# The last product of a three-layer kernel, computed by Strassen's algorithm in pairs of token tiles

## The chip, the cores and the metric

The kernel runs on one core of a Trainium2 chip. The metric is device time in microseconds, the median of 3 runs. One execution was profiled; times inside it are counted from its first instruction. PE is the matmul engine, PEld its weight loads, DVE, ACT and POOL the three engines for elementwise work, SP the engine that issues nearly all DMAs.

## The reference

Three layers follow each other. Here is what they compute, with shapes:

```python
# q, k, v: (4, 8, 576, 64)
kv  = einsum('bhsd,bhse->bhde', k, v)
o   = einsum('bhsd,bhde->bhse', q, kv)
x   = o / sqrt(mean(o*o) + 1e-6) * g_norm            # -> (2304, 512) tokens
h   = x @ w_in                                       # (512, 1024)
s   = h * softmax(h)
x   = layernorm(s) * g_ln @ w_out                    # (1024, 512)
out = ((x @ w_a) * (x @ w_b)) @ w_out2               # (512,1536) twice, (1536,512)
```

The last line is the part that concerns us: a = x @ w_a, b = x @ w_b, and the output product (a*b) @ w_out2 with 2304 tokens, 1536 inner columns and 512 output columns.

## The kernel before

All arithmetic is in float32. A matmul operand is split into a high part (rounded to the type fp32r by an ACT cast) and a low part (the rest, by a subtraction on DVE or POOL), and a product is three matmuls: high by high, high by low, low by high.

The products a and b run in units called quads (`quad`, L726). The 2304 tokens are three blocks s of 768 (SB = 6 tiles of 128), the 1536 inner columns are 6 groups j of 256, and m says whether a or b is made. A quad already uses Strassen's algorithm: a 2 by 2 arrangement of half blocks is multiplied by 7 products (`product`, L706, 6 matmuls of 384 columns each) and 15 sums and differences instead of 8 products. The sums of x and of the weights are made beforehand; the sums of results are the `add` calls on DVE. The seventh product of a quad is issued within the next quad (`close_quad`), after that quad's third. In m = 1 the results are multiplied with those of m = 0 (`times`, mostly on POOL) and stored to DRAM in `gd[s]`.

The output product (`mm_out`, L824) is plain. For each of 18 token tiles it accumulates 12 chunks of 128 inner columns, three matmuls each, into one PSUM bank of 512 columns: 36 matmuls, 648 in all. The token tile is the stationary operand, the weight w_out2 (512 columns) the moving one. Its operands come back from `gd` two tiles at a time (`g_fetch`), and are split by one ACT cast and one DVE subtraction of 1536 columns for each tile (`g_steps`). The weight is loaded and split during the last four quads (`wo_steps`, as side steps).

Nothing reorders the program: each engine executes its instructions in the order in which the Python code issues them. A quad calls `tick` after six of its products. At each tick it issues a share of a list of side steps (`side`) and whatever `delayed` holds for that tick, so that work which is not the quad's own is placed between its own instructions. An instruction that waits holds up everything behind it on its engine; a DMA that waits holds up SP's later DMAs. `first_place`, `second_place` and `last_place` take over memory of tiles that are no longer needed.

PSUM has six banks for these stages; a quad uses three (b1, b2, b3) and hands them to the next but one.

Of the kernel before, what the change touches and what calls it, by code (L numbers as in the profile page):

```python
# [19 lines left out]
P = 128  # L20
# [79 lines left out]
def tile_attention_moe(ctx, tc, q, k, v, g_norm, w_in, w_out, g_ln, w_a, w_b, w_out2, out):  # L100
# [58 lines left out]
    pool("lp", 1).tile([P, 168], F32, name="lp")  # L159
# [8 lines left out]
    ring = xl0.tile([P, 7 * TB // 2], I64, tag="x", name="ring")  # L168
# [72 lines left out]
    def put_w2(f, eng, c):  # L241
        nc.sync.dma_start(out=w2d[c], in_=f)
# [331 lines left out]
    def x_begin(s):  # L574

        t = xl0.tile([P, 7, 2, TH], F32, tag="x", name="xf")
        x_load(s, [t[:, n] for n in (XB11, XT3, XB21, XB22)])

        def minus(out, a, b):
            return lambda: subtract(nc.vector, t[:, out], t[:, a], t[:, b])  # L580
# [32 lines left out]
    def stage():  # L613

        t = xl0.tile([P, 7 * TB // 2], I64, tag="x", name="st")
        st.update(wr=t[:, :2 * DM], wu=t[:, 2 * DM:3 * DM], ws=t[:, 3 * DM:3 * DM + 3 * P], e=t[:, 3 * DM + 3 * P:])
# [109 lines left out]
    def quad(j, s, m, side=()):  # L726
# [23 lines left out]
        def times(n, by, eng):  # L750

            eng.tensor_tensor(out=a[n], in0=by, in1=a[n], op=ALU.mult)  # L752
            i, h = n // 10 - 1, n % 10 - 1
            nc.sync.dma_start(out=gd[s][:, j, i, h * TH:(h + 1) * TH], in_=a[n])
# [31 lines left out]
        def close():  # L786
            product(b3, w, x, WA22, XT4, False, True)
            add(t[21], b3)
            if m:
                times(21, t[21], nc.gpsimd)  # L790
# [3 lines left out]

    wo2 = {}

    def wo_fetch(c, t):
        for k in range(2):
            wo2[c + k] = t[:, k, 0], t[:, k, 1]
            nc.sync.dma_start(out=t[:, k, 1].bitcast(F32), in_=w2d[c + k])  # L800

    def wo_steps(c, eng):
        return [
            lambda: nc.scalar.copy(wo2[c][0], wo2[c][1].bitcast(F32)),
            lambda: subtract(eng, wo2[c][1], wo2[c][1].bitcast(F32), wo2[c][0].bitcast(F32)),
        ]

    graw = {}
    gs = {}

    def g_fetch(s, n, t=None):
        if t is None:
            t = p2["gr"].tile([P, NF2, 2 * P], F32, tag="gr", name="gr")
        nc.sync.dma_start(
            out=t, in_=gd[s].rearrange("p j i t -> p (j i) t")[:, :, n * 2 * P:(n + 1) * 2 * P]
        )
        graw[s, n] = t

    def g_steps(s, n, h, where, tag="gs"):
        t = where.tile([P, 2, NF2, P], F32R, tag=tag, name="gs")  # L820
        hi, lo = gs[s, n, h] = t[:, 0], t[:, 1]
        return split_steps(hi, lo, graw[s, n][:, :, h * P:(h + 1) * P], nc.vector)

    def mm_out(s, n, h, within=None):  # L824
        hi, lo = gs.pop((s, n, h))
        po = banks["pool"].tile([P, 512], F32, tag="t", name="pq")

        order = [(k, c) for c in range(NF2) for k in range(3)]
        if within:
            order.sort(key=lambda kc: kc[0] == 2)  # L830
        for i, (k, c) in enumerate(order):
            if within and i == 12:
                within()
            wh, wl = wo2[c]
            x, w = ((hi, wh), (hi, wl), (lo, wh))[k]
            nc.tensor.matmul(po, x[:, c], w, start=(i == 0), stop=(i == len(order) - 1))  # L836
        o = p2["o"].tile([P, DM], F32, tag="o", name="o_sb")
        nc.scalar.copy(o, po)  # L838
        a = 0
# [231 lines left out]
```

## Time and profile before

| | us |
|---|---|
| median of 3 runs (lowest, highest) | 725.02 (724.25, 727.12) |
| the profiled execution | 724.55 |
| its span, first to last instruction | 722.8 |
| PE busy in the span | 693.4 (96%) |
| DVE, ACT, POOL busy | 421.4, 269.1, 298.4 |

A matmul's time in a row is its whole passage through the array; consecutive matmuls overlap, so the pace of PE is read from the distance between starts. The shares of the other engines are averages over stages that differ much.

### The profile page before, as it was taken

The page shows a single profiled execution, that of the slowest core. Times are in us where ns is not written, and L with a number is a line of the kernel's source. Part 1 is how long each engine was busy: PE and PEld are TensorE (multiplying, and loading weights), DVE is VectorE, ACT ScalarE, POOL GpSimd, SP SyncE. Part 2 cuts the span into 40 slices and gives each one's busy share as a digit, 9 for nine tenths or more (in the row PEclk, how much of TensorE's full clock was granted, in tenths as well). Part 3 has the DMA queues.
Part 4 walks back from the last instruction along what each step waited for, and adds up shares of the span by engine and source line. Part 5 has one row for each costly group of instructions (what it writes and reads, how often), then busy time and mean ns, then how long its engine had stood idle before and what let it go on. Part 6 is the DMA issues. An engine that isn't in the chain of part 4 may idle for free.

```text
span 722.8 us, 10923 instructions
## 1 busy us (share of the span) xinstructions
PE 693.4 (96%) x4064; PEld 636.1 (88%) x4064; DVE 421.4 (58%) x767; ACT 269.1 (37%) x456; POOL 298.4 (41%) x445
## 2 busy tenths in 40 slices
PE   3699999999999999999999999999999899999998
PEld 2578898998998998899999999999999788888886
DVE  3888977765688777777764565645645521221110
ACT  4558864443553346443221212223113322222230
POOL 2588776677657220124357444665444300000000
PEclk9899999999999999999999999999999999999999
DMA  9976545445532411351333331343115474433301
GB/s 295 310 229 186 186 121 181 120 131 165 164 110 67 143 41 53 116 165 56 132 112 124 114 103 55 102 135 104 44 71 196 161 250 151 147 117 116 117 34 39
DMA packets 93236, 95.08 MB, mean 132 GB/s; under 512 B 28416, under 2 KB 82688, under 8 KB 93184
## 3 DMA queue, kind: packets, MB, share of 16 engines
q1 hardware_dynamic: 88000, 89.67, 39.1%
q10 hardware_dynamic: 5184, 4.72, 1.9%
q8 instruction: 32, 0.52, 0.3%
q14 instruction: 20, 0.16, 0.1%
HBM read 65.54 MB, written 28.84 MB: 131 GB/s over the span
## 4 chain that ended last, share of the span: by engine, by line
PE 77%; DVE 7%; POOL 5%; DMA 5%; issue 4%; ACT 2%; SPq 1%; ACTq 0%; POOLq 0%; DVEq 0%
PE pw L711 27%; PE pq L836 20%; PE x2p L529 4%; PE x2p L528 4%; PE x2p L527 4%; PE ph L440 3%; PE ph L442 3%; PE ph L441 3%; PE ltp L497 2%; PE kvp L344 2%; PE po L378 1%; DMA vr<-in_v_dram 1%; DMA both<-gd 1%; POOL a L752 1%; DMA ks<-in_k_dram 1%
## 5 line engine op out<-in xcount | busy, mean ns | idle before, releaser
L711 PE MATMUL pw<-xh,wh 128*128 128x384 f32 x504 | 170.0, 337 | 1.5 <-DVE b L741 0.8
L711 PE MATMUL pw<-xh,wl 128*128 128x384 f32 x504 | 168.5, 334 | 0.0
L711 PE MATMUL pw<-xl,wh 128*128 128x384 f32 x504 | 168.5, 334 | 0.0
L836 PE MATMUL pq<-wq,gs 128*128 128x512 f32 x540 | 125.8, 389 | 2.0 <-ACT gs L558 2.0
L836 PEld LDWEIGHTS pq<-wq,gs 128*128 128x128 f32 x540 | 101.3, 188 | 23.2 <-ACT gs L558 2.3
L752 POOL TENSOR_TENSOR a<-b,a 128x384 f32<-128x384 f32 x54 | 60.9, 1140 | 120.9 <-DVE b L741 75.7
L711 PEld LDWEIGHTS pw<-xh,wh 128*128 128x128 f32 x504 | 94.6, 188 | 5.6 <-DVE b L741 2.7
L711 PEld LDWEIGHTS pw<-xl,wh 128*128 128x128 f32 x504 | 94.6, 188 | 0.0
L711 PEld LDWEIGHTS pw<-xh,wl 128*128 128x128 f32 x504 | 94.6, 188 | 0.0
L554 DVE TENSOR_TENSOR gs<-gr,gs 128x1536 fp32r<-128x1536 f32 x16 | 28.1, 1759 | 99.7 <-ACT gs L558 99.7
L527 PE MATMUL x2p<-lh,woh 128*128 128x256 f32 x288 | 82.4, 286 | 0.2 <-ACT lh L507 0.2
L528 PE MATMUL x2p<-ll,woh 128*128 128x256 f32 x288 | 80.4, 279 | 0.7 <-DVE ll L510 0.7
L529 PE MATMUL x2p<-lh,wol 128*128 128x256 f32 x288 | 80.4, 279 | 0.5 <-DVE wol L49 0.5
L442 PE MATMUL ph<-wih,xl 128*128 128x512 f32 x144 | 56.4, 392 | 1.4 <-DVE xl L425 1.4
L440 PE MATMUL ph<-wih,xh 128*128 128x512 f32 x144 | 57.0, 396 | 0.0
L441 PE MATMUL ph<-wil,xh 128*128 128x512 f32 x144 | 56.2, 391 | 0.4 <-DVE wil L49 0.4
L528 PEld LDWEIGHTS x2p<-ll,woh 128*128 128x128 f32 x288 | 54.1, 188 | 1.1 <-DVE ll L510 1.1
L527 PEld LDWEIGHTS x2p<-lh,woh 128*128 128x128 f32 x288 | 54.1, 188 | 0.8 <-ACT lh L507 0.5
L529 PEld LDWEIGHTS x2p<-lh,wol 128*128 128x128 f32 x288 | 54.0, 188 | 0.9 <-DVE wol L49 0.9
L66 POOL TENSOR_SCALAR nu<-nu 128x512 f32<-128x512 f32 x23 | 44.2, 1931 | 20.6 <-ACT nu L61 19.7
L838 ACT COPY o_sb<-pq 128x512 f32<-128x512 f32 x18 | 10.6, 588 | 107.3 <-issue 86.8
L741 DVE TENSOR_TENSOR a<-pw,a 128x384 f32<-128x384 f32 x54 | 29.7, 554 | 31.0 <-PE pw L711 30.9
(123 smaller groups left out, 1158.4 us busy)
## 6 DMA issues: line engine op xcount, KB each, us to landing
gd<-a SPq DMA_DIRECT2D x72, 192.0 KB, 1.8
gr<-gd SPq DMA_DIRECT2D x8, 1536.0 KB, 6.9
ring<-in_moe_w_out_dram SPq DMA_DIRECT2D x20, 512.0 KB, 5.4
ks<-in_k_dram SPq DMA_DIRECT2D x8, 512.0 KB, 7.0
vs<-in_v_dram SPq DMA_DIRECT2D x8, 512.0 KB, 7.6
ring<-in_moe_w_in_dram SPq DMA_DIRECT2D x8, 512.0 KB, 6.6
qs<-in_q_dram SPq DMA_DIRECT2D x16, 256.0 KB, 6.6
x2d<-x2s ACTq DMA_DIRECT2D x32, 128.0 KB, 1.8
```

Source lines behind the costliest of these rows:

```text
L66: eng.tensor_scalar(out=u, in0=u, scalar1=2.0 ** -15, scalar2=122879.9921875, op0=ALU.max, op1=ALU.min)
L440: nc.tensor.matmul(ph[:, n, :], xh[:, c, :], wh, start=(c == 0), stop=False)
L441: nc.tensor.matmul(ph[:, n, :], xh[:, c, :], wl, start=False, stop=False)
L442: nc.tensor.matmul(ph[:, n, :], xl[:, c, :], wh, start=False, stop=(c == NK - 1))
L527: nc.tensor.matmul(pa, wh[:, cs], lh[:, f, :], start=(f == 0), stop=False)
L528: nc.tensor.matmul(pa, wh[:, cs], ll[:, f, :], start=False, stop=False)
L529: nc.tensor.matmul(pa, wl[:, cs], lh[:, f, :], start=False, stop=(f == NF1 - 1))
L554: eng.tensor_tensor(out=out, in0=a, in1=b, op=ALU.subtract)
L711: nc.tensor.matmul(out, wt_[:, wn, c], xt_[xn][:, c], start=first and c == n == 0, stop=c == 1 and n == 2, skip_group_check=not first,)
L741: nc.vector.tensor_tensor(out=t, in0=ps, in1=t, op=ALU.add)
L752: eng.tensor_tensor(out=a[n], in0=by, in1=a[n], op=ALU.mult)
L836: nc.tensor.matmul(po, x[:, c], w, start=(i == 0), stop=(i == len(order) - 1))
```

## The change

The output product is now also computed by Strassen's algorithm. Two token tiles that lie 384 tokens apart in a block form a pair (9 pairs). The inner columns are halved by the two 128-column chunks of each j (6 chunks per half), the output columns into 256 and 256. A pair is 7 products of 6 chunks by 3 matmuls of 256 columns (`out_product`): 126 matmuls, 1134 in all. The results are joined by five DVE sums and two ACT copies per pair (`out_pair`).

The pair's operands are four loads, four differences and seven splits of 128x768 (`g_steps`); in pair k those of pair k + 1 are made, three or two steps at each of seven ticks. A load for pair k + 2 is issued right after the product of pair k that used the same memory. The sums of the weight's quarters (`w2_sums`, 4 per j) are made on DVE in six earlier quads and stored to DRAM. `gd` is laid out by quarter, so a store is three runs of 512 bytes per partition where it was one of 1536. The operands of the first pair are loaded and split during the last six quads in two pieces (`most`: 5 of the 6 chunks, `last`: the sixth); in the first pair its own last operands, the last weights and all of pair 1's operands are made.

```diff
+    def w2_sums(j, eng=nc.vector):
+        def step(n, a, b, op=ALU.subtract):
+            return lambda: eng.tensor_tensor(out=w2e_[j][:, n], in0=w2e_[j][:, a], in1=w2e_[j][:, b], op=op)
...
+        return [step(4, 2, 3, ALU.add), step(5, 4, 0), step(2, 0, 2), step(1, 1, 5), keep]
+    def g_load(k, n, c=slice(0, NJ), t=None):
+        s, m = pairs[k]
+        t = g2[k, n][1].bitcast(F32) if t is None else t
+        nc.sync.dma_start(out=t[:, c], in_=gd[s][:, (XB11, XT3, XB21, XB22).index(n), m, c])
+    def g_split(k, n, src, c=slice(0, NJ)):
+        return [
+            lambda: nc.scalar.copy(g2[k, n][0][:, c], src()[:, c]),
+            lambda: subtract(nc.vector, g2[k, n][1][:, c], src()[:, c], g2[k, n][0][:, c].bitcast(F32)),
+        ]
+    def g_steps(k):
...
+        return [
+            begin_, *sp(XB11), d(1, XB22, -1), *sp(XT1, 0), d(0, XB21, -2), *sp(XT2, 1), d(1, XB22, XT3),
+            *sp(XB21), *sp(XB22), *sp(XT3, 1), *sp(XT4, 0),
+        ]
+    def out_product(ps, k, wn, xn, first):
+        (wh, wl), (xh, xl) = wo2[wn], g2[k, xn]
+        for c in range(NJ):
+            for n, (xt_, wt_) in enumerate(((xh, wh), (xh, wl), (xl, wh))):
+                nc.tensor.matmul(
+                    ps, xt_[:, c], wt_[:, c], start=first and c == n == 0, stop=c == NJ - 1 and n == 2,
+                    skip_group_check=not first,
+                )
+    def out_pair(k, side, begin_=lambda: None):
...
+        b1 = bank_()
+        mm(b1, WA11, XB11, True)
+        begin_()
...
+        nc.scalar.copy(c21, b1)
+        tick()
+        b2 = bank_()
+        mm(b2, WS1, XT1, True)
+        add(c22, b2, c21)
+        tick()
+        b3 = bank_()
+        mm(b3, WS2, XT2, True)
+        add(c12, b3, c21)
+        close_quad()
+        tick()
+        mm(b1, WA12, XB21, False)
+        nc.scalar.copy(c11, b1)
+        tick()
+        mm(b2, WS4, XB22, False)
+        add(c12, b2)
+        tick()
+        mm(b3, WS3, XT3, False)
+        add(c22, b3)
+        store(1)
+        tick()
+        def close():
+            mm(b3, WA22, XT4, False)
+            add(c21, b3)
+            store(0)
...
     for j in range(1, NJ - 1):
         n = 2 * j + 2
-        quad(j, 0, 0, w_split(3, nc.vector) if j == 1 else ())
+        quad(j, 0, 0, w_split(3, nc.vector) if j == 1 else w2_sums(order.pop(0)))
...
-        quad(j, 2, 0, w_sums(n + 1))
+        quad(j, 2, 0, [*w_sums(n + 1), *(w2_sums(order.pop(0)) if j > 1 else ())])
...
+    then(
+        t1=early[10:12], t3=[first_place, wl(WA11, w1, 0)],
+        t4=[gl_(XB11, last), gl_(XT3, last), gl_(XB22, last), wl(WS1, w1, 1)], t5=[gl_(XB21, last)],
+    )
+    quad(j, 2, 0)
...
+    def last_places():
+        close_quad()
+        all_of([*half(WS4, 1), *half(WS3, 0)])
+        ab.close()
+        p2["o"] = pool_r("o", 5)
+        p2["e"] = pool_r("e", 1)
...
+        for n in (XB11, XT3, XB22, XB21):
+            g_load(1, n)
+        wo_load(WA22, None, w2[6])
...
+    first = [
+        *half(WS3, 1), *g_steps(1), *g_split(0, XT4, lambda: te[:, 0]), last_hi,
+        *half(WA22, 0, nc.gpsimd), *half(WA22, 1, nc.gpsimd),
+    ]
+    for k in range(len(pairs)):
+        out_pair(k, *((g_steps(k + 1) if k + 1 < len(pairs) else [],) if k else (first, last_places)))
```

How the instructions now stand is shown for three places. First PE in the output stage before, from the second part of the first tile on (`gs` is the split token tile, `wq` and `both` hold the weight):

```order
L836 MATMUL pq<-wq,gs 128x512 x8
L836 MATMUL pq<-both,gs 128x512 x4
L836 MATMUL pq<-wq,gs 128x512 x10
L836 MATMUL pq<-both,gs 128x512 x2
L836 MATMUL pq<-wq,gs 128x512 x30
L836 MATMUL pq<-both,gs 128x512 x6
L836 MATMUL pq<-wq,gs 128x512 x30
```

And PE in the output stage now, from the second product of the first pair on (`ga`, `gw`, `gxh` are token operands, `wo` weights; L886 is the matmul of `out_product`):

```order
L886 MATMUL pq<-wo_6122,ga 128x256 x18
L886 MATMUL pq<-wo_6122,gw 128x256 x18
L886 MATMUL pq<-wo_6269,gw 128x256 x54
L886 MATMUL pq<-wo_6122,gxh 128x256 x54
L886 MATMUL pq<-wo_6548,gw 128x256
L886 MATMUL pq<-wo_6269,gw 128x256
L886 MATMUL pq<-wo_6548,gw 128x256 x2
```

Each tile's 36 matmuls of 512 columns became, for two tiles, seven products of 18 matmuls of 256 columns; the first pair's seventh product (the row with `wo_6548` and those after it) stands after the second pair's third.

Second DVE at the turn from the last quad to the output stage, before (L741 and L752 are a quad's own sums and product, L554 the splits; in brackets the semaphores that an instruction waits for):

```order
L554 TENSOR_TENSOR gs<-both,gs 128x1536 [waits DMAHW5_49,Activation_49]
L741 TENSOR_TENSOR b_6237<-pw,b_6237 128x384 [waits DVE_49,PE_49]
L554 TENSOR_TENSOR both<-both 128x512 [waits DMAHW6_49,Activation_49]
L741 TENSOR_TENSOR b_6239<-pw,b_6239 128x384 [waits PE_49]
L741 TENSOR_TENSOR b_6238<-pw,b_6238 128x384 [waits PE_49,Pool_49]
L554 TENSOR_TENSOR gs<-both,gs 128x1536 [waits Activation_49]
L554 TENSOR_TENSOR gs<-gr,gs 128x1536 [waits DMAHW4_49,Activation_49]
L554 TENSOR_TENSOR gs<-gr,gs 128x1536 [waits Activation_49]
L554 TENSOR_TENSOR gs<-gr,gs 128x1536 [waits DMAHW5_49,PE_49,Activation_49]
```

And DVE there now (L745 and L756 are the last quad's sum and product, L557 splits and differences, L908 the pair's sums; `gxh`, `gxl` are pair 1's operands, `e` its differences, `o` the output tile):

```order
L745 TENSOR_TENSOR b_6301<-pw,b_6301 128x384 [waits PE_49,Pool_49]
L756 TENSOR_TENSOR a_6230<-b_6301,a_6230 128x384 [waits DVE_49]
L557 TENSOR_TENSOR wo_6269<-wo_6269 128x768 [waits Activation_49]
L557 TENSOR_TENSOR wo_6269<-wo_6269 128x768 [waits DMAHW0_49,Activation_49]
L557 TENSOR_TENSOR wo_6269<-wo_6269 128x768 [waits Activation_49]
L557 TENSOR_TENSOR e_6424<-gxl,gxh 128x768 [waits DMAHW4_49,DMAHW3_49,DMAHW5_49,DMAHW2_49,DMAHW6_49,DMAHW1_49,DMAHW7_49,DVE_49,Pool_49]
L908 TENSOR_TENSOR o_6420<-pq,o_6419 128x256 [waits PE_49]
L557 TENSOR_TENSOR gxh<-gxh 128x768 [waits DVE_49,Activation_49]
L557 TENSOR_TENSOR e_6425<-gxl,e_6424 128x768 [waits DMAHW0_49]
L557 TENSOR_TENSOR gxh<-e_6424,gxh 128x768 [waits Activation_49]
L908 TENSOR_TENSOR o_6420<-pq,o_6419 128x256 [waits PE_49]
```

Where DVE had one split per tile and nothing else, it now makes pair 1's operands; the difference into `e_6424`, which waits for loads, stands ahead of the first pair's own sum into `o_6420`.

Third SP's queue there, before:

```order
L754 DMA gd_78<-a_6166 128x384 [waits DMAHW0_49,DVE_49]
L754 DMA gd_78<-a_6167 128x384 [waits DMAHW1_49,Pool_49]
L754 DMA gd_78<-a_6169 128x384 [waits DMAHW2_49,Pool_49]
L754 DMA gd_78<-a_6168 128x384 [waits DMAHW3_49,Pool_49]
L814 DMA gr<-gd_79 128x12x256 [waits DMAHW4_49,PE_49]
L814 DMA gr<-gd_79 128x12x256 [waits DMAHW5_49]
```

And now (L758 is the store of `times`, L834 `g_load`, L828 `wo_load`):

```order
L758 DMA gd_67<-a_6228 128x3x128 [waits DMAHW1_49,DVE_49]
L758 DMA gd_67<-a_6229 128x3x128 [waits DMAHW2_49,Pool_49]
L758 DMA gd_67<-a_6231 128x3x128 [waits DMAHW3_49,Pool_49]
L834 DMA ga<-gd_68 128x768 [waits DMAHW4_49,PE_49]
L758 DMA gd_67<-a_6230 128x3x128 [waits DMAHW5_49,DVE_49]
L834 DMA gxh<-gd_68 128x768 [waits DMAHW6_49,PE_49]
L834 DMA gxl<-gd_68 128x768 [waits DMAHW7_49]
L834 DMA gxl<-gd_68 128x768 [waits DMAHW0_49]
L834 DMA gxl<-gd_68 128x768 [waits DMAHW1_49]
L828 DMA wo_6269<-w2d 128x1536 [waits DMAHW2_49]
```

The four loads of pair 1 (`gxh`, `gxl`) stand behind the last store of the last quad, `a_6230`, which waits for DVE; before, two loads of twice the tokens stood there.

## Rows read from the trace of the kernel before

**Rows 1.** The chain that ended last, shares of the span by engine and line, from the page.

```profile
PE pw L711 27%; PE pq L836 20%; PE x2p L529 4%; PE x2p L528 4%; PE x2p L527 4%; PE ph L440 3%; PE ph L442 3%; PE ph L441 3%; PE ltp L497 2%; PE kvp L344 2%; PE po L378 1%; DMA vr<-in_v_dram 1%; DMA both<-gd 1%; POOL a L752 1%; DMA ks<-in_k_dram 1%
```

**Rows 2.** Stretches of 29 to 144 us: busy time of each engine, granted clock.

```profile
core 0: us, PE busy (x) PEld busy (x) DVE busy (x) ACT busy (x) POOL busy (x), PEclk, DMA share, GB/s
495.00:539.00 44.00, 43.85 (x252) 43.23 (x251) 23.61 (x44) 9.03 (x15) 23.80 (x22) 1.00 0.23 80
539.00:568.30 29.30, 29.30 (x170) 29.12 (x168) 16.15 (x28) 8.50 (x16) 10.67 (x9) 1.00 0.60 204
...
574.90:719.10 144.20, 144.20 (x637) 119.22 (x636) 30.93 (x18) 33.59 (x34) 2.38 (x3) 1.00 0.36 123
```

**Rows 3.** PE in time (start us, us), start of the output stage, the wait before it.

```profile
567.93 0.33 PE L711 MATMUL pw<-xl,wh 128*128 128x384 f32 x1
568.10 0.34 PE L711 MATMUL pw<-xh,wl 128*128 128x384 f32 x1
570.42 3.02 PE L836 MATMUL pq<-wq,gs 128*128 128x512 f32 x12 [1.98 <-ACT gs L558]
573.74 0.44 PE L711 MATMUL pw<-xh,wh 128*128 128x384 f32 x1 [0.31 <-DVE b L741]
...
574.89 2.01 PE L836 MATMUL pq<-wq,gs 128*128 128x512 f32 x8
...
580.38 6.96 PE L836 MATMUL pq<-wq,gs 128*128 128x512 f32 x30
...
588.53 6.96 PE L836 MATMUL pq<-wq,gs 128*128 128x512 f32 x30
```

**Rows 4.** The last instructions of PE and ACT, in time.

```profile
717.74 1.52 PE L836 MATMUL pq<-both,gs 128*128 128x512 f32 x6
719.34 0.59 ACT L838 COPY o_sb<-pq 128x512 f32<-128x512 f32 x1 [7.57 <-PE pq L836]
```

**Rows 5.** PE in time, 256-column matmuls of an earlier stage: first and last of 95.

```profile
277.34 0.28 PE L528 MATMUL x2p<-ll,woh 128*128 128x256 f32 x1
...
288.41 0.28 PE L529 MATMUL x2p<-lh,wol 128*128 128x256 f32 x1
```

**Rows 6.** Weight loads of the output stage, by line and form: busy us, mean ns of one.

```profile
L836 PEld LDWEIGHTS pq<-wq,gs 128*128 128x128 f32 x540 | 101.3, 188 | 23.2 <-ACT gs L558 2.3
```

**Rows 7.** Groups by line and form, DVE, ACT and POOL: busy us, mean ns of one.

```profile
L741 DVE TENSOR_TENSOR b<-pw,b 128x384 f32<-128x384 f32 x54 | 29.8, 555 | 15.2 <-PE pw L711 15.2
L554 DVE TENSOR_TENSOR gs<-gr,gs 128x1536 fp32r<-128x1536 f32 x16 | 28.1, 1759 | 99.7 <-ACT gs L558 99.7
...
L554 POOL TENSOR_TENSOR wl<-st,wh 128x768 fp32r<-128x768 f32 x8 | 14.8, 1850 | 0.0
...
L588 ACT CAST xh<-xf 128x768 fp32r<-128x768 f32 x14 | 11.0, 834 | 1.7 <-ACT b L537 1.2 <-POOL w0s L554 0.5
...
L554 DVE TENSOR_TENSOR wl<-st,wh 128x768 fp32r<-128x768 f32 x2 | 3.0, 1514 | 2.0 <-ACT wh L689 2.0
...
L554 DVE TENSOR_TENSOR xl<-xl,xh 128x768 fp32r<-128x768 f32 x3 | 2.8, 947 | 0.0
...
L554 DVE TENSOR_TENSOR st<-xl 128x768 f32<-128x768 f32 x2 | 2.6, 1305 | 0.1
```

**Rows 8.** DMAs by tile: KB each, median us from issue to landing.

```profile
gd<-a SPq DMA_DIRECT2D x72, 192.0 KB, 1.8
gr<-gd SPq DMA_DIRECT2D x8, 1536.0 KB, 6.9
```

**Rows 9.** The tile gr: spread of the landing times of its 8 loads.

```profile
DMA to landing us min/median/max: 6.7/6.9/10.2
```

**Rows 10.** DVE in time, the same split once while POOL works and once alone.

```profile
576.66 2.23 DVE L554 TENSOR_TENSOR gs<-both,gs 128x1536 fp32r<-128x1536 f32 x1 [0.94 <-ACT gs L558]
586.00 1.76 DVE L554 TENSOR_TENSOR gs<-gr,gs 128x1536 fp32r<-128x1536 f32 x1 [7.10 <-ACT gs L558]
```

**Rows 11.** POOL in time around the first of these.

```profile
576.27 1.01 POOL L752 TENSOR_TENSOR a<-b,a 128x384 f32<-128x384 f32 x1
```

More of the change, by code (lines that the diff above doesn't have):

```diff
@@ L789, in close, with w2_load @@
             if m:
-                times(21, t[21], nc.gpsimd)
+                times(21, t[21], nc.vector if (j, s) == (NJ - 1, 0) else nc.gpsimd)
         open_quad.append(close)
+    HD = DM // 2
     wo2 = {}
[L797 to L802, printed above, removed]
+    g2 = {}
+    def w2_load(j):
+        w2e_[j] = st["e"].bitcast(F32).rearrange("p (n d) -> p n d", n=6)
+        nc.sync.dma_start(out=w2e_[j][:, :4], in_=w2d[:, :4, j])
@@ L824, in mm_out @@
[L824 to L839, printed above, removed]
-        for b, c0, rows in tiles[s * SB + 2 * n + h]:
-            nc.sync.dma_start(out=out[b * S + c0:b * S + c0 + rows, :], in_=o[a:a + rows, :])
-            a += rows
+            lambda: nc.scalar.copy(g2[k, n][0][:, c], src()[:, c]),
@@ L897, in tile_attention_moe @@
     rest = ExitStack()
+    pairs = []
     run(PROLOGUE)
@@ L1030, in tile_attention_moe, with place @@
-    quad(j, 0, 1, [*side[16:20], *[lambda: None] * 2, *g_steps(*todo[0], p2["x2"], "xl"), *side[20:]])
-    mm_out(*todo[0], last_place)
-    for k, now in enumerate(todo[1:], 1):
-        if k + 1 < len(todo):
-            all_of(g_steps(*todo[k + 1], p2["gs"]))
-            if todo[k + 1][2] and k > 1 and loads:
-                g_fetch(*loads.pop(0))
-        mm_out(*now)
+        parts(w2, p2["x2"].tile([P, 14 * TB + 32], F32R, tag="x", name="wo2"), 7)
+    def place(where, tag):
+        t = where.tile([P, 2, NJ, P], F32R, tag=tag, name="gw")
+        return t[:, 0], t[:, 1]
@@ new lines, in tile_attention_moe @@
+    for n, k in ((XB11, 0), (XT1, 1)):
+        g2[0, n] = ga[:, k, 0], ga[:, k, 1]
+    g2[0, XB21], g2[0, XB22] = (place(p2["w", part, 0], "w") for part in "hl")
+    most, last = slice(0, NJ - 1), slice(NJ - 1, NJ)
+    early, late_ = g_first(most), g_first(last)
+    then(
+        t1=[gl_(XB11, most), gl_(XT3, most)], t4=[gl_(XB22, most), gl_(XB21, most)], t6=early[:3],
+    )
+    quad(j, 1, 0)
+    then(t1=early[3:4], t2=early[4:6], t3=early[6:7], t4=early[7:8], t5=early[8:10])
+    quad(j, 1, 1)
```

201 lines of the change are left out of this document (142 added, 59 removed).

## The prediction

> **What bounds the kernel now.** I read the chain of waits first: 20% of the span is PE in the output stage (line 836) and 27% PE in the quads [rows 1]. Then the table by stretches, because shares over the whole span mix stages. In the output stage (574.9 to 719.1) PE is busy for the whole 144.2 us at full clock, DVE for 31 and ACT for 34; in the last quads before it (539.0 to 568.3) PE is busy all 29.3 us, DVE 16.2 [rows 2]. So PE's pace sets the end, and a change of the number or the width of matmuls is felt one to one as long as the others keep up. The reader is to see there that DVE has 113 us to spare in the output stage; the change spends most of it. Last I read PE in time around the turn from quads to output stage [rows 3] and the end [rows 4].
>
> **PE's work in the output stage.** A matmul row of 512 columns lasts longer than its pace: 36 of them start at 580.38 and the next 36 at 588.53, so one takes 8.15/36 = 0.2264 us [rows 3]; the 636 from 574.89 on fill the 144.2 us of the stage's stretch [rows 2], 0.2267 each, which I take. Before: 648 x 0.2267 = 146.9 us. Now 1134 of 256 columns. The output stage of before has none, but an earlier stage has the same shape and type (128x128 stationary, 256 columns moving): 95 starts from 277.34 to 288.41, 11.07/94 = 0.1178 us [rows 5]. Now: 1134 x 0.1178 = 133.6 us. Term: -13.3 us. Bounds for the price of one: from above the 384-column pace of the quads, 0.173 (567.93 to 568.10) [rows 3], which would be 196.2 us; from below half of a 512-column matmul, 0.1134, which would be 128.6 us (-18.3). I take 0.1178, since it is the only row with the same operation.
>
> The rule that speaks against the change: the Trainium skill, "TensorE: Matmul & The Clock Gate", section "Back-to-back issue gap", gives a sustained spacing of about 81 ns at 128 columns and 131 ns at 512 in a stream of weight loads and matmuls. On a line between these, 256 columns would cost 98 ns, 0.75 of a 512-column matmul, and 1.75 times as many matmuls would be 1.3 times the stage. The rows disagree with it: 0.2267 for 512 [rows 3] and 0.1178 for 256 [rows 5], a ratio of 0.52. By the rows the sum is -13.3, by the rule's ratio about +45. I follow the rows; the mechanism is the third rival.
>
> **The turn before.** The last matmul of the last quad's sixth product starts at 568.10, the first of the output stage at 570.42, waiting for ACT's cast of the first tile; 0.173 of that is the matmul, 2.15 is stall. At 573.74 the leftover product waits again: 12 matmuls of 0.2267 from 570.42 would be followed at 573.14; the product's first matmul starts 0.6 later, of which 0.31 is shown as idle; I take 0.47 [rows 3]. These 2.6 us go, since the first pair's first operands are now made in the quads before. What is late next is worked out below.
>
> **The turn now.** Let T be the start of the first pair's first product. A product takes 18 x 0.1178 = 2.12. PE: first product to T+2.1, the last quad's seventh (6 x 0.173 = 1.04) to T+3.2, second to T+5.3, third to T+7.4, fourth to T+9.5. DVE makes the quad's last sum and product (two of 0.55, 384 columns [rows 7]) by T+4.3; behind that product stand SP's store and then the four loads of pair 1, issued from about T+4.6. Price of a load of 384 KB: the loads of 1536 KB land after 6.7 at best and 10.2 at worst [rows 9], which I read as the second of the two that stood back to back in SP's queue; it adds 3.5 plus the time between their issues, some 4.3 in all for 1536 KB, so an estimate of 1.1 for 384 KB, and 2.4 is fixed. Pair 2's first load stands in front, but is issued 2 us earlier. The first two land at about T+8.1 and T+9.2. Until then DVE has three weight splits (3 x 0.9, to T+7) and waits.
>
> The wait is new, and it stands ahead of the sum that frees the second bank. Price of a DVE step of 128x768: half of 1759 is 0.88; the same shape took 0.947; with others beside it 1.305 and 1.514 [rows 7]. I take 0.9, the rows nearest to an idle POOL. So the first difference ends at T+10.1, the second bank's sum (256 columns, 0.35 to 0.42) at T+10.5; PE wanted it at T+9.5: stall 1.0. Three more steps and the third bank's sum end at T+13.6; PE wants it at T+12.7: 0.9. Pair 0's seventh product needs the last weight, whose halves POOL splits (1850 ns each [rows 7]) after ACT's cast, by about T+23 against T+22.9: 0.1. Sum +2.0. Bounds: from below 0 (loads landing by T+8 end both waits); from above a landing 10.2 after issue [rows 9], T+14.8 in place of T+9.2, +7.6.
>
> POOL's work beside DVE has a price: the same 1536-column split took 2.23 while POOL worked and 1.76 alone [rows 10, 11]. The Trainium skill, "GPSIMD Engine Reference", section "1. Specifications", says that POOL's SBUF interfaces are shared with DVE and that they contend when a DVE instruction has two SBUF inputs; all of a pair's differences and splits have two. The trace agrees, 1.27 times. By the rule and the row pair 1's steps lengthen for the 3.7 us of POOL's two splits, by 0.8, inside the slack counted next, so the sum is the same.
>
> **The other pairs.** PE needs 126 x 0.1178 = 14.8 us a pair. DVE has four differences and seven splits, 11 x 0.9 = 9.9, and five sums of 0.42, 12.0 in all. ACT has seven casts of 0.834 [rows 7] and two copies, under 7 us. Loads are issued half a pair or more ahead of their use, except one: the last of the four is issued when the pair's sixth product ends, and the next pair's first difference needs it about 2.3 us later, when DVE gets there; it lands after 3.5, so DVE idles about 1 us per pair. 13 of 14.8: hidden. Cost 0; bounds 0 and, at 1.514 a step, (11 x 1.514 + 2.1 - 14.8) x 9 = +36.
>
> **Quads before.** The sums of the weight (24 on DVE, at most 0.5 each, and 18 stores and 6 loads on SP's queue) fall in quads where DVE is busy 24 of 44 us [rows 2]. In the last six quads DVE has 33 sums and products at 0.55, nine splits at 0.9 and sixteen smaller steps, 34 of 43.8 us, with loads to wait for. A quad's sum has about 2 us before PE wants its bank. I work out one place with little cover: the first weights' load stands on SP behind a store that waits for POOL (about 6 us into that quad) and lands 5 us later, 1.5 us after DVE reaches its split. One microsecond of the 2 is left, so no stall. I put 0.5 for all of it; bounds 0 and 4 (each of the four waits for loads late by one more). The stores to `gd` have shorter runs; they land in 1.8 before [rows 8], and nothing waits for one sooner than a quad later but the reuse of memory at the turn, covered by the waits counted above.
>
> **The end.** Before, ACT copies 512 columns in 0.59 after the last matmul [rows 4]; now DVE sums 256 in 0.4: -0.2. The store behind it stays.
>
> **Sum.** -13.3 - 2.6 + 2.0 + 0.1 + 0.5 - 0.2 = -13.5 against the execution's own 724.55: 711.0. The runs' median is 0.5 above that execution, so 711.5.
>
> **Rivals.**
> First, the turn costs more: loads land late, the memory of the quads' results is freed late (pair 0's outputs lie where those were), and both banks' sums slip. For it: eight waits on one DVE instruction, in front of PE's next bank. Against it: the loads' own rows. Price: the upper bounds, 7.6 instead of 2.0 at the turn and 2 more in the quads: 711.5 + 7.6 = 719.
>
> Second, slower: DVE becomes the bound of the output stage. Place: every pair's seven splits and four differences. It decides from the step price at which nine pairs cost what the stage costs now, 146.9 + 2.6 + 0.2 - 2.6 = 147.1, or 16.3 a pair: (16.3 - 2.1)/11 = 1.30 us a step. The rows have 1.305 and 1.514 for this shape [rows 7]; at 1.514 the stage is 9 x 18.8 = 169 us, time 725 + 22 = 747. Against it: POOL is idle in that stage [rows 2], and alone the split ran at 1.145 ns per column [rows 7].
>
> Third, slower too: narrow matmuls aren't cheaper in proportion, because each has its own weight load of 188 ns [rows 6], longer than the 118 ns. It decides from 147.1/1134 = 0.130 us; at the 384-column pace 0.173 the time is 711.5 + 62.6 = 774. Against it: in the 256-column rows the same load is hidden [rows 5].
>
> Fourth, better: the matmuls at half of 512 (0.1134) and no stall at the turn, 711.5 - 5.0 - 2.0 = 704.5.
>
> **Chances.** Forecast (turn and quads cost 0 to 4.5): 0.65, and its own range 709 to 714. First rival 0.22 (714 to 721). Second 0.06, half of it milder and still faster or the same, half slower. Third 0.02. Fourth 0.05. A measurement of this kernel tells a change of 0.5%, 3.6 us, from none. Faster by that means below 721.4: 0.65 + 0.05 + 0.20 = 0.90; within: 0.05; slower: 0.05. The range that should hold the time 8 times in 10 takes in the forecast and most of the first rival: 707 to 719.
>
> **What would show it.** In the changed profile: about 1134 matmuls of 256 columns with starts 0.118 apart, and the stage from first to last of them 133 to 140 us. At the turn, PE idle before the first pair's fifth and sixth products, released by DVE's sums, in all 1 to 4 us, and the difference into `e` waiting for a DMA; no gap like the 2.15 at its start. Nine equal pairs of 14.8 us with no PE idle from the third on; DVE busy 75 to 90% there. PE idle released by DVE within every pair would show the second rival, starts 0.13 or more apart the third. I am wrong if quads before the turn lengthen by more than 2 us, or if gaps at the turn exceed 5.

## The result, and the profile after

The changed kernel takes 716.2 us (median; 715.7 to 719.0) where the kernel before took 724.6 (723.6 to 727.1) on the same chip: ratio 0.9886, interval 0.9851 to 0.9922. The forecast was 711.5, with a range of 707 to 719. The profiled execution is 716.3 us with a span of 714.5; before, 724.55 and 722.8. So the span is 8.3 us shorter, where the working said 13.5.

Where PE had nothing to wait for, the stage is what was worked out. PE in time, changed kernel, pair 2 and later (L886 is the matmul of `out_product`):

```profile
597.70 6.52 PE L886 MATMUL pq<-wo,gxl 128*128 128x256 f32 x54
604.06 4.40 PE L886 MATMUL pq<-wo,ga 128*128 128x256 f32 x36
```

54 starts take 604.06 - 597.70 = 6.36 us, 0.1178 each, as in [rows 5]. The table by stretches, to be read beside [rows 2]:

```profile
core 0: us, PE busy (x) PEld busy (x) DVE busy (x) ACT busy (x) POOL busy (x), PEclk, DMA share, GB/s
...
539.00:566.70 27.70, 26.50 (x148) 25.21 (x147) 19.85 (x36) 9.70 (x18) 6.02 (x6) 1.00 0.62 203
566.70:597.00 30.30, 24.35 (x183) 23.34 (x182) 23.85 (x26) 13.59 (x20) 12.04 (x6) 0.94 0.62 203
579.30:583.20 3.90, 3.81 (x19) 3.81 (x20) 2.53 (x4) 2.03 (x4) 0.00 (x0) 0.56 1.02 415
597.00:708.00 111.00, 111.00 (x944) 110.90 (x942) 83.72 (x116) 42.31 (x63) 0.00 (x0) 1.00 0.42 118
```

From 597 to 708 PE has no gap, and DVE is busy 83.7 of 111 us, 75%. Nearly all that went wrong lies in the second row, the turn (PE 24.4 of 30.3 us busy), and in the first, the last quads, which were full before [rows 2]. The turn in time, changed kernel, all engines, without the rows that change nothing:

```profile
565.46 8.81 SPq L758 DMA_DIRECT2D gd<-a  x3
...
565.65 1.57 ACT L874 CAST wo<-wo 128x768 fp32r<-128x768 f32 x2 [4.39 <-DMA wo<-w2d]
...
566.56 4.35 POOL L557 TENSOR_TENSOR wo<-wo 128x768 fp32r<-128x768 f32 x2 [6.09 <-ACT wo L874]
566.59 0.33 PE L715 MATMUL pw<-xh,wl 128*128 128x384 f32 x1
...
566.76 2.20 PE L886 MATMUL pq<-wo,ga 128*128 128x256 f32 x18
567.12 0.83 ACT L838 CAST gw<-te 128x768 fp32r<-128x768 f32 x1
...
567.98 1.24 DVE L557 TENSOR_TENSOR gw<-te,gw 128x768 fp32r<-128x768 f32 x1 [2.55 <-ACT gw L838]
569.15 1.01 DVE L745 TENSOR_TENSOR b<-pw,b 128x384 f32<-128x384 f32 x2
570.08 1.65 DVE L557 TENSOR_TENSOR wo<-wo 128x768 fp32r<-128x768 f32 x1
...
570.21 0.44 PE L715 MATMUL pw<-xh,wh 128*128 128x384 f32 x1 [1.25 <-DVE b L745]
...
570.87 3.02 POOL L756 TENSOR_TENSOR a<-b,a 128x384 f32<-128x384 f32 x2
...
572.23 0.79 DVE L756 TENSOR_TENSOR a<-b,a 128x384 f32<-128x384 f32 x1
...
573.40 2.32 PE L886 MATMUL pq<-wo,gw 128*128 128x256 f32 x18
574.37 0.44 SPq L834 DMA_DIRECT2D ga<-gd  x1
574.90 0.40 SPq L758 DMA_DIRECT2D gd<-a  x1
575.40 0.44 SPq L834 DMA_DIRECT2D gxh<-gd  x1
575.88 1.51 SPq L834 DMA_DIRECT2D gxl<-gd  x3
...
578.97 0.37 ACT L924 COPY o<-pq 128x256 f32<-128x256 f32 x1 [8.62 <-DMA gd<-a]
...
579.39 0.95 PE L886 MATMUL pq<-wo,gw 128*128 128x256 f32 x4 [3.67 <-DMA gxh<-gd]
```

To be read backwards. PE waits until 579.39. Its row names a load, but the matmul there is the fourth product, which goes into the bank that ACT's copy at 578.97 empties, 0.42 earlier. That copy had waited 8.62 us for the stores of the quad's results (`gd<-a`), since the output tile lies in memory that these free. SP issued the stores late: three of them hold its queue for 8.81 us, as POOL makes its last two products only at 570.87, behind its two splits of WA12, the weight of the fourth product. The four loads of pair 1 stand behind them and go out from 575.40, 8.6 us after the first product's start, where I had 4.6. Against [rows 3]: the first product follows the quad without a gap (566.59, 566.76), so the old stall of 2.15 is gone.

The wait of 1.25 at 570.21, before the quad's seventh product, begins on ACT. Its two casts of WA12 (565.65) waited 4.39 us for that weight's load. Behind them stands the cast of a token operand (567.12), behind that DVE's subtraction (567.98), and behind that DVE's last sums of the quad (569.15), for which PE waits. POOL's two products need the same sums.

And the long wait costs twice: after it the granted clock is 0.56 (third row of the table by stretches), mostly the lower of the two levels (1.2 of 2.4 GHz). Eighteen matmuls start 0.213 apart in place of 0.118: 1.7 us.

The last pair, changed kernel, beside [rows 4]:

```profile
706.77 1.34 PE L886 MATMUL pq<-wo,gw 128*128 128x256 f32 x10
...
708.14 0.42 DVE L908 TENSOR_TENSOR o<-pq,o 128x256 f32<-128x256 f32 x1 [1.70 <-PE pq L886]
...
708.62 2.38 PE L886 MATMUL pq<-wo,gw 128*128 128x256 f32 x18 [0.52 <-DVE o L908]
711.04 0.42 DVE L908 TENSOR_TENSOR o<-pq,o 128x256 f32<-128x256 f32 x1 [2.48 <-PE pq L886]
```

The sixth and the seventh product use the same bank. In the other pairs the next pair's products lie between them; in the last none does, so the seventh waits for the sixth's sum.

### The profile page after: what moved, and what is told of

Same layout as the page of the kernel before. It is cut to its first block, busy times and chain, and to the rows that moved or that the text cites. A ratio compares the mean times of both kernels' runs of the same rounds, so it can differ in the third digit from the quotient of the medians.

```text
span 714.5 us, 12258 instructions
## 1 busy us (share of the span) xinstructions
PE 681.2 (95%) x4550; PEld 648.6 (91%) x4550; DVE 520.7 (73%) x928; ACT 292.4 (41%) x507; POOL 306.4 (43%) x444
## 5 line engine op out<-in xcount | busy, mean ns | idle before, releaser
L756 POOL TENSOR_TENSOR a<-b,a 128x384 f32<-128x384 f32 x53 | 63.5, 1211 | 124.0 <-DVE b L745 123.0
L715 PE MATMUL pw<-xh,wh 128*128 128x384 f32 x336 | 114.2, 340 | 1.9 <-DVE b L745 1.4
L715 PE MATMUL pw<-xh,wl 128*128 128x384 f32 x336 | 112.9, 336 | 0.0
L715 PE MATMUL pw<-xl,wh 128*128 128x384 f32 x336 | 112.9, 336 | 0.0
L715 PE MATMUL pw<-x,wh 128*128 128x384 f32 x336 | 85.6, 335 | 1.0 <-DVE b L745 0.6
L886 PE MATMUL pq<-wo,gw 128*128 128x256 f32 x522 | 65.9, 285 | 5.2 <-DMA gxh<-gd 3.7
L886 PEld LDWEIGHTS pq<-wo,gw 128*128 128x128 f32 x522 | 64.0, 192 | 6.2 <-ACT o L924 3.9
L715 PEld LDWEIGHTS pw<-xh,wh 128*128 128x128 f32 x336 | 63.1, 188 | 5.5 <-DVE b L745 3.1
L715 PEld LDWEIGHTS pw<-xl,wh 128*128 128x128 f32 x336 | 63.1, 188 | 0.0
L715 PEld LDWEIGHTS pw<-x,wh 128*128 128x128 f32 x336 | 60.6, 188 | 1.9 <-DVE b L745 0.9
L715 PE MATMUL pw<-x,wl 128*128 128x384 f32 x168 | 56.2, 334 | 0.0
```

Of the source, the lines that this page charges most:

```text
L715: nc.tensor.matmul(out, wt_[:, wn, c], xt_[xn][:, c], start=first and c == n == 0, stop=c == 1 and n == 2, skip_group_check=not first,)
L886: nc.tensor.matmul(ps, xt_[:, c], wt_[:, c], start=first and c == n == 0, stop=c == NJ - 1 and n == 2, skip_group_check=not first,)
```

## The experiments

Each was timed in turn with the kernel before on one chip (the first four on one, the next three on another, the last three on a third). "Stage" is the time from the first to the last start of an output matmul in the profile: 144.0 in the changed kernel, where 133.6 + 1.0 for the quad's seventh product, 134.6, would be without a wait. Before it is 148.5, or 150.6 with the stall of 2.15 ahead of it. "From the quads" is from the first matmul of the quads to the end of the span: 434.2 before, 429.6 changed. The expectations call DVE VectorE, ACT ScalarE and SP SyncE.

**POOL's splits behind its products.**

```diff
-        t3=[*half(WA12, 0, nc.gpsimd), *half(WA12, 1, nc.gpsimd)],
         t4=[last_operands, *g_split(0, XT3, lambda: te[:, 2])],
-        t6=half(WS4, 0),
+        t6=[*half(WA12, 0, nc.gpsimd), *half(WA12, 1, nc.gpsimd), *half(WS4, 0)],
```

> The changed kernel, but POOL's two splits of the fourth weight (WA12) are issued after POOL's two products of the last quad instead of ahead of them; no other work is moved. Theory (POOL's queue): at the turn the stores of the last quad stand behind these products, these behind 4.4 us of splits that wait for a late weight load; the output tile's memory and the loads of pair 1 wait for the stores. Then stores are issued 4 to 5 us earlier, the 3.7 us wait before the first pair's fourth product and the stretch at half clock behind it (1.7 us) go, and the 1.4 us wait before the last quad's seventh product shrinks; about 2 us of waiting for pair 1's loads is left. From the stage's first to last matmul 144.0 falls to 138 to 139.5, time 716.2 to about 711. Rival (the loads of pair 1 themselves are slow, 3.7 to 6.4 us): the wait moves to the fifth product, the stage stays at 142 or more, time 714.5 or more.

713.0 us, ratio 0.983 (0.979 to 0.986), stage 139.2: the stage as the theory had it, the time 2 us above it (the quads start at 286.4 in this profile, 1.4 us later than in the changed kernel's). The turn in time, this kernel:

```profile
565.41 0.84 ACT L838 CAST gw<-te 128x768 fp32r<-128x768 f32 x1 [2.41 <-PE pw L715]
...
567.97 0.55 DVE L745 TENSOR_TENSOR b<-pw,b 128x384 f32<-128x384 f32 x1
...
568.65 2.00 POOL L756 TENSOR_TENSOR a<-b,a 128x384 f32<-128x384 f32 x2 [6.42 <-DVE b L745]
...
574.07 0.44 SPq L834 DMA_DIRECT2D gxh<-gd  x1
...
575.86 0.37 ACT L924 COPY o<-pq 128x256 f32<-128x256 f32 x1 [3.44 <-DMA gd<-a]
...
576.28 2.39 PE L886 MATMUL pq<-wo,gw 128*128 128x256 f32 x18 [0.33 <-ACT o L924]
...
579.97 2.39 PE L886 MATMUL pq<-wo,gw 128*128 128x256 f32 x18 [1.29 <-DVE o L908]
```

The first product starts at 568.51 here; the loads go out 5.6 us after it, not 8.6, the copy waits 3.4 us, not 8.6, the wait before the quad's seventh product is gone, and the gaps there are 0.5, 1.5 and 0.7 us. The clock stays at its upper level. The stage is 4.8 us shorter.

The edit moves more than POOL's work, though: each `half` is a cast on ACT and then a subtraction on POOL, so ACT's two casts of WA12 go back as well. The token cast that stood behind them is now made at 565.41, 3.1 us ahead of the first output product instead of 0.4 behind its start, and DVE's first sum at 567.97, 0.5 ahead instead of 2.4 behind. POOL's products start 0.1 us after the first output product, where they started 4.1 after it; the first sum that they need was ready only 2.9 after it, so POOL's own splits held them for an estimated 1.2 us, and the rest came with ACT's casts. The run shows that the splits of WA12, on both engines, held the turn; how much of the 4.8 us belongs to each engine it does not show.

**Own memory for the first pair's output tiles.**

```diff
-        o = [p2["o"].tile([P, DM], F32, tag="o", name=f"o{h}") for h in range(2)]
+        o = p2.pop("o0", None) or [p2["o"].tile([P, DM], F32, tag="o", name=f"o{h}") for h in range(2)]
...
+        p2["o0"] = [te[:, n].rearrange("p j t -> p (j t)")[:, :DM] for n in (1, 2)]
```

> The changed kernel, but the first pair's two output tiles lie in memory of the differences (te) that is free by then, not where the last quad's results lie; all else as it was. By the theory of POOL's queue the fourth product no longer waits, but DVE's first difference still waits for loads that SP issues behind the same stores, so the wait moves on to the fifth product, until about 16 us after the stage's start: stage 143 to 144, time 715 to 716.5. By the rival that the reuse of memory alone makes the wait, the stage falls by 4 us or more, time 712 or less.

717.1 us, 0.989 (0.986 to 0.993), stage 143.3. The fourth product now runs on, and the whole wait stands before the fifth:

```profile
573.39 4.44 PE L886 MATMUL pq<-wo,gw 128*128 128x256 f32 x36
582.25 5.91 PE L886 MATMUL pq<-wo,gw 128*128 128x256 f32 x31 [4.42 <-DVE te L908]
```

That the memory alone was the matter is refuted: behind the copy stands DVE's sum, held by the loads in SP's queue. The copy's wait went and the time stayed: both waits have one cause.

**The last pair's sixth product before its fifth.**

```diff
...
+        steps = [fifth, sixth] if k + 1 < len(pairs) else [sixth, fifth]
...
```

> The changed kernel, but the last pair's sixth product (third bank) stands ahead of its fifth (second bank), so that DVE's sum of the third bank is not between two products that follow each other. Theory: the 0.7 us gap before the very last product goes, all else stays: time 715.5, ratio to before 0.987 to 0.988. Rival: the gap is only moved to the end (the sums run behind the last matmul anyway): no change.

718.4 us, 0.990 (0.987 to 0.994): within the scatter of the changed kernel itself, so the time settles nothing. The profile does settle the wait: the last 57 matmuls run on in one row, and the gap of 0.7 is gone.

```profile
707.78 6.86 PE L886 MATMUL pq<-wo,gw 128*128 128x256 f32 x57
```

**The kernel before, once more.**

> The kernel before, unchanged, for its own spread: ratio 1.000. In the two profiles so far the quads start 3.6 us earlier in the changed kernel (285.0 against 288.5), though hardly anything differs ahead of them. If that is the spread of one execution (landing of the first loads), this profile's quads start anywhere between 285 and 289; if it comes from the change, they start within 0.5 us of 288.5 again.

725.5 us, ratio 1.001 (0.998 to 1.003). From the quads 433.0; the quads start at 289.2, 0.7 us later than in its first profile and far from the changed kernel's 285.0.

**The early layout alone, in the kernel before.** The changed kernel also stores the second weight by quarters and splits an early buffer in two:

```diff
-    w2d = [dram.tile([P, DM], F32, name=f"w2d{f}") for f in range(NF2)]
+    w2d = dram.tile([P, 7, NJ, DM // 2], F32, name="w2d")
...
-    ring = xl0.tile([P, 7 * TB // 2], I64, tag="x", name="ring")
+    ring = [xl0.tile([P, n * TB // 2], I64, tag=f"x{n}", name="ring") for n in (4, 3)]
```

> The kernel before, with one thing of the changed kernel: where the early parts lie (one tensor in device memory for the second block's weights, stored by quarters, and the first operand buffers split in two). The output stage keeps its seven-product-free, 512-column form. Theory A: the 2 to 4 us that the changed kernels are ahead of the kernel before at the start of the quads come from this layout. Then the quads start at about 286 us in the profile and the time is about 722 us. Theory B: that start differs from one execution to the next (285 to 289.4 us were seen in kernels of both kinds) and the layout is worth nothing. Then the time is within 1 us of the kernel before, 724 to 725.5 us, and the start falls anywhere from 285 to 289.5.

724.5 us where the kernel before took 726.3: 0.998 (0.996 to 1.000). Quads start at 289.7. Theory A falls: in this profile the layout does not bring the early start.

**The last quads spread, and the last pair's order.** On top of the first experiment and the third:

```diff
-        t2=half(WA11, 0), t3=[wl(WS2, w1, 2), *late_[:4]], t4=half(WA11, 1), t5=late_[4:8], t6=late_[8:],
+        t3=[wl(WS2, w1, 2), *half(WA11, 0), *late_[:4]], t4=late_[4:8], t5=late_[8:], t6=half(WA11, 1),
...
-        t1=half(WS1, 0), t2=half(WS1, 1), t3=[second_place, wl(WA12, w2, 0)], t4=half(WS2, 0),
-        t5=[wl(WS4, w2, 1), *half(WS2, 1)], t6=[wl(WS3, w2, 2), *g_split(0, XT2, lambda: te[:, 1])],
+        t2=half(WS1, 0), t3=[second_place, wl(WA12, w2, 0)], t4=half(WS1, 1),
+        t5=[wl(WS4, w2, 1)], t6=[wl(WS3, w2, 2), *half(WS2, 0)],
...
+        t1=half(WS2, 1), t2=g_split(0, XT2, lambda: te[:, 1]),
```

> The changed kernel with POOL's splits of WA12 put behind its products (as in the run before), the last pair's sixth product before its fifth, and VectorE's splits of WA11, WS1, WS2 and XT2 spread one or two steps later over the last quads. Theory: the gaps of 0.66, 0.76, 0.36 and 0.18 us in the last quads are VectorE's backlog behind a split of WA11 whose load lands late; with the splits later they go, 1.5 to 2 us, and 0.7 us go with the gap before the last product: 710 to 711 us where the kernel with POOL's work put last alone took 713. Rival: VectorE is short of time in that stretch as a whole, so that what moves later delays the turn to the output stage by as much: gaps of 1.5 us or more appear at the first pair's first products and the time stays at 712 to 713 us.

710.1 us, 0.979 (0.976 to 0.982), as the theory had it. The waits of the last quads in the changed kernel were these; here PE has no gap there but one of 0.27 us:

```profile
549.39 0.62 PE L715 MATMUL pw<-x,wh 128*128 128x384 f32 x2 [0.45 <-DVE b L770]
...
554.42 0.62 PE L715 MATMUL pw<-x,wh 128*128 128x384 f32 x2 [0.57 <-DVE b L745]
```

From the quads' start to the end of their matmuls ahead of the first output product: 279.7 us before, 281.8 changed, 280.5 here. What is left at the turn is now the wait that I had predicted (DVE in time, this kernel):

```profile
577.48 0.96 DVE L557 TENSOR_TENSOR e<-gxl,gxh 128x768 f32<-128x768 f32 x1 [0.92 <-DMA gxl<-gd]
578.35 0.42 DVE L908 TENSOR_TENSOR o<-pq,o 128x256 f32<-128x256 f32 x1
```

The first difference of pair 1 waits for its load, and the first pair's own sum stands behind it; PE waits 1.8 us and then 0.7.

**The loads on ACT's queue, own memory, WA22 earlier.** On top of the last kernel, with the second experiment's memory for the output tiles (WA22 is the weight of the seventh product):

```diff
-            g_load(1, n)
+            g_load(1, n, eng=nc.scalar)
...
+    *most_steps, s1, s2 = g_steps(1)
     first = [
-        *half(WS3, 1), *g_steps(1), *g_split(0, XT4, lambda: te[:, 0]), last_hi,
-        *half(WA22, 0, nc.gpsimd), *half(WA22, 1, nc.gpsimd),
+        *half(WS3, 1), *most_steps, *g_split(0, XT4, lambda: te[:, 0]), last_hi,
+        *half(WA22, 0, nc.gpsimd), *half(WA22, 1, nc.gpsimd), s1, s2,
```

> The kernel of the run with the last quads spread, and in the first pair: its output tiles in memory that is free already, pair 1's four loads issued on ScalarE's queue in place of SyncE's, and POOL's split of WA22 asked for two VectorE steps earlier. Theory: what is left of the turn (1.46 + 0.71 + 0.65 us of gaps) comes from loads that stand in SyncE's queue behind POOL's stores and from WA22's split; off that queue they go, about 2 us: 708 to 709 us. Rival: the loads wait for memory that the last quad's results free, not for the queue; then they land as late as before, the gaps stay and the time is that of the kernel without this part within 0.5 us; or ScalarE, which issues them, is held by that wait and its casts come late, 711 to 713 us.

712.7 us, 0.981 (0.978 to 0.985): a median 2.6 us above the kernel without this part. Of the difference in the two profiles hardly anything lies in the part that was edited: the quads start at 288.4 here and at 286.4 there, and from the quads on the two take 423.6 and 423.2. So the theory's gain of 2 us did not come, and no loss is shown either. The gaps of the turn are one of 3.6 us, with the lower clock behind it, in place of several. Memory decides, as the rival had it, though in another place. The loads went out 3.3 us after the first product's start, not 5.8, and so ahead of the last store. The store's landing, this kernel's tile `a` in 572 to 576 us, and then the same of the kernel without the edit:

```profile
DMA to landing us min/median/max: 6.1/6.1/6.1
```

```profile
DMA to landing us min/median/max: 2.0/2.0/2.0
```

And `e`, the target of pair 1's first difference, lies in memory that this store frees:

```profile
580.32 0.96 DVE L557 TENSOR_TENSOR e<-gxl,gxh 128x768 f32<-128x768 f32 x1 [1.99 <-DMA gd<-a]
581.20 0.42 DVE L908 TENSOR_TENSOR te<-pq,te 128x256 f32<-128x256 f32 x1
```

It begins 11.6 us after the first product, where it began 10.5 after it without this edit. Sending the loads ahead of the store gained nothing.

**Sums free of the wait.** The kernel with the last quads spread, in another order of the first pair's steps:

```diff
+    *most_steps, s1, s2 = g_steps(1)
     first = [
-        *half(WS3, 1), *g_steps(1), *g_split(0, XT4, lambda: te[:, 0]), last_hi,
-        *half(WA22, 0, nc.gpsimd), *half(WA22, 1, nc.gpsimd),
+        *half(WS3, 1), *g_split(0, XT4, lambda: te[:, 0]), last_hi, *[lambda: None] * 5, *most_steps,
+        *half(WA22, 0, nc.gpsimd), *half(WA22, 1, nc.gpsimd), s1, s2,
```

> The kernel of the run with the last quads spread (710 us), with one thing more: the first pair's list of VectorE steps is in another order. Pair 1's sums, which wait for its loads, come one product later (empty steps and the split of XT4, which waits for nothing, take their place), and POOL's split of WA22 is asked for two steps earlier. All loads stay on SyncE's queue and the output tiles where they are. Theory: the gaps of 1.79 and 0.71 us in the first pair are the sums of the first pair's results standing behind pair 1's sums on VectorE, which wait for the loads of gxl, and the 0.64 us is WA22's split: all three go, the one of 0.59 us (ScalarE's copy waits for the output tile's memory) stays, and the time is 707 to 707.5 us. Rival: VectorE has too many steps left after the loads have landed, so that the wait turns up in pair 1: gaps of 1.5 us or more between 585 and 597 us and 709 to 710 us.

709.3 us, 0.978 (0.975 to 0.980), the lowest time; stage 137.4, where it was 138.9 without this edit. The two intervals overlap, so the gain rests on the profiles. The time is the rival's, the cause is not: the 1.8 became 0.8, the 0.7 went, but the wait for WA22 grew from 0.6 to 1.3: POOL ends its split 24.0 us after the first product's start (584.92 + 4.59 - 565.56), 1.6 us sooner than without the edit, and PE would have been there at 22.7, 2.2 sooner. PE in time:

```profile
573.43 2.38 PE L886 MATMUL pq<-wo,gw 128*128 128x256 f32 x18 [0.43 <-ACT o L924]
576.44 4.35 PE L886 MATMUL pq<-wo,gw 128*128 128x256 f32 x36 [0.62 <-DVE o L908]
589.57 1.21 PE L886 MATMUL pq<-wo,gw 128*128 128x256 f32 x8 [1.17 <-POOL wo L557]
```

**Both layouts in device memory, in the kernel before.** As the layout experiment, and `gd` by quarter, with four loads for one:

```diff
...
-            nc.sync.dma_start(out=gd[s][:, j, i, h * TH:(h + 1) * TH], in_=a[n])
...
+            nc.sync.dma_start(out=gd[s][:, at_, :, j], in_=a[n].rearrange("p (m t) -> p m t", t=P))
...
```

> The kernel before with the early layout of the changed kernel and its layout of the gated tokens in device memory; the old output product reads them with four loads in place of one. Everything ahead of the quads then moves the same bytes through the same instructions as in the changed kernel. Theory A: the layouts in device memory give the changed kernels their faster start; the quads start at 285 to 286.5 us and the first 36 us move 307 to 315 GB/s. Theory B: the start doesn't hang on it; the quads start at 288.5 to 289.7 us, the first 36 us move 280 to 301 GB/s, as in the three profiles of the form before. The output stage itself may lose up to 3 us by the smaller loads (chances: A 0.3, B 0.7).

723.0 us where the kernel before took 724.9: 0.998 (0.996 to 1.000). Quads start at 288.0, half a microsecond ahead of theory B's range and 1.5 behind theory A's, and the first 36 us move 293 GB/s, inside B's: theory B.

**The changed kernel, once more.**

> The changed kernel as it is, on the same chip as the other two. By the first measurement 716 us, ratio 0.986 to 0.991 to the kernel before; its quads start at 285 to 286.5 us if the faster start belongs to it, at 288 to 289.5 us in about one execution of three if that varies. From the quads' start to the end 429 to 430 us, with the half clock after the long gap again if that follows from the gap.

717.4 us, 0.990 (0.987 to 0.993); quads start at 285.3, from there 430.0 to the end, the long gap 3.8 us again with matmuls at the lower clock behind it.

## Why the prediction came out as it did

The time fell inside the range, but not in the forecast's own 709 to 714: it is in the first rival's 714 to 721. Both signs by which the forecast called itself wrong came about: the quads are 2.1 us longer (its limit was 2), and the gaps at the turn add up to 6.8 (its limit was 5). And luck kept the time inside the range. The kernel was 3.6 us ahead when the quads began, which no term speaks of; without that lead it would have been at about 719.8, past the upper end, or, by the mean lead of all profiles (2.5, below), at 718.7, just inside it. By terms, us, from the two profiles:

| Term | Predicted | Measured | From |
|---|---|---|---|
| PE's matmuls | -13.3 | -13.3 | pace 0.1178 where nothing waits |
| old stall at the turn | -2.6 | -2.6 | first product follows without a gap |
| turn now | +2.1 | +8.5 | gaps 1.41, 3.84, 0.64, 0.23, 0.64, and 1.7 at the lower clock |
| other pairs | 0 | +0.7 | the last pair's seventh product |
| quads | +0.5 | +2.1 | 279.7 to 281.8 |
| end | -0.2 | -0.1 | 718.87 to 722.76, 710.73 to 714.51 |
| ahead of the quads | 0 | -3.6 | they start at 284.96, not 288.53 |
| sum | -13.5 | -8.3 | |

The predicted +2.1 holds 0.1 too much: the sum of +2.0 for the turn already had the 0.1 of the last weight in it, and it was added once more.

*Matmuls.* Right, and the third rival is refuted. The Trainium skill ("TensorE: Matmul & The Clock Gate", "Back-to-back issue gap") gives spacings from which, as an estimate, 256 columns would cost 0.75 of 512; that does not hold here: 0.1178 against 0.2267. It was right to take the row with the same operation.

*The other pairs.* Right for seven of eight. DVE is busy 74.6 of 90 us from 600 to 690, 83%, where I had 12.0 of 14.8, 81%, and its step took 0.95; the second rival, with its 1.30, is refuted. The last pair I had not looked at by itself: its seventh product has no other pair's products in front. The third experiment's profile shows it.

*The turn now: the step that failed.* "DVE makes the quad's last sum and product by T+4.3; behind that product stand SP's store and then the four loads of pair 1, issued from about T+4.6." SP's queue holds three more stores ahead of that one, and two of these are of POOL's products. On POOL they stand behind the two splits of WA12, 4.35 us, themselves waiting for a load; and the sums that they need were late on DVE, since ACT's casts of WA12 waited 4.39 us for the same load. So the loads went out at T+8.6. The order that I read showed those stores waiting for POOL; I counted DVE's part alone, and even that came at T+6.3 (572.23 + 0.79 - 566.76), not T+4.3. With the splits of WA12 moved behind, ACT's part and POOL's, the loads go at T+5.6 and the wait of DVE's sums is 1.5 and 0.7, near the 1.0 and 0.9 predicted: the mechanism was right, its start was not. My first rival named the place and both causes (loads late, memory freed late), at up to 7.6; the measured 8.5 is beyond even that, and holds two things that it does not name: 1.7 for the clock, and 1.4 before the quad's seventh product.

*Quads.* "One microsecond of the 2 is left, so no stall": wrong. The load of the first weights landed 4.9 us after issue as I had it, but the split behind it put DVE's next sums late, and the lateness was passed on from sum to sum: gaps of 0.6, 0.7, 0.3 and 0.2. With the splits one or two steps later they went. I had added up the busy time and looked at one wait; the sums of a row of steps that each have 2 us to spare can still be late in turn.

*Ahead of the quads.* Nothing in my sum speaks of it. Eight profiles of kernels with the new output stage start the quads at 285.0 to 289.4 us, mean 286.4; four with the old one at 288.0 to 289.7, mean 288.9. Medians say the same: the kernel with both layouts took 723.0 and the changed one 717.4 on one chip, of which only 432.0 - 430.0 lies behind the quads' start. It begins with the first transfers. DMA in the first 36 us, the changed kernel and then the kernel with both layouts:

```profile
DMA packets 13245, 11.27 MB, mean 313 GB/s; under 512 B 7929, under 2 KB 11964, under 8 KB 13244
```

```profile
DMA packets 12383, 10.55 MB, mean 293 GB/s; under 512 B 7728, under 2 KB 11102, under 8 KB 12382
```

All eight move 307 to 318 GB/s there, all four 281 to 301, with the same instructions in that stretch. Two of the eight still start their quads at 288.4 and 289.4, having lost their lead later; in the latter, the kernel with the last pair reordered, the granted clock is 0.53 from 31 to 42 us, where the changed kernel's is 1.00. The kernel with both layouts has the changed kernel's instructions on every engine up to the quads and not its start, so the layouts do not bring it; what does, stays open. So of the 8.3 us, the change's own part from the quads on is about 4, by its two profiles 429.6 and 430.0 against 434.2 and 433.0 before.

The versions show that the forecast was within reach: with the turn and the quads mended, 709 to 710 us. From the quads to the end, free of the early start, the best profile takes 421.5 us, where 434.2 - 13.5 makes 420.7.

## What to carry to other kernels

When a queue holds an instruction that you count on, walk every entry ahead of it back to its engine's own queue, ACT's and POOL's too: the splits of one late weight on two engines with time to spare cost 4.8 us, because sums and products stood behind them, and stores and loads behind those. Sum a stage by its pace, but walk its first and its last round in time, since the cover that holds in the middle (another pair's products, a load half a pair ahead) is missing there. And check how much of a measured gain lies in the stretch that was changed before you credit the change with it.

## What the runs showed of the hardware

- After PE had stood still for 3.6 to 4.6 us, its matmuls ran at the lower clock level for some us: granted clock 0.56 after 3.8 us (above), 0.50 after 4.6 in the kernel with own memory (582.2 to 586.6), and 0.67 after 3.6 in the kernel with ACT's loads:

```profile
581.60:585.00 3.40, 3.33 (x19) 3.33 (x20) 3.40 (x6) 2.17 (x4) 0.00 (x0) 0.67 0.23 91
```

  After gaps of 1.5 us (the first experiment) and 1.8 it stayed up (the kernel with the last quads spread, after 1.79):

```profile
578.80:581.00 2.20, 2.18 (x18) 2.18 (x18) 2.20 (x3) 1.01 (x2) 0.00 (x0) 1.00 1.02 412
```

- While POOL worked, DVE's steps of 128x768 took 1.24 and 1.65 where they take 0.95 alone, and POOL's products beside DVE took 1.5 in the changed kernel where they took 1.0 in the first experiment (the rows of the two turns above): more than the 1.27 of [rows 10, 11], and in both directions.
- A store of 192 KB that landed in 2.0 us took 6.1 when four loads, 1.5 MB in all, had been issued on another queue in the 2.1 us ahead of it (the kernel with ACT's loads).
